# The first attention unit as a function of its own: 64x64 score tiles, a Q and a K tile per level, and K on ScalarE's DMA queue

## The chip, the cores and the metric

The kernel runs on one core of one Trainium2 chip. The metric is the device time of one execution in microseconds (us); the median of several runs counts. Engines are called as the profile calls them: PE (TensorE, its matmuls), PEld (its weight loads), DVE (VectorE), ACT (ScalarE), POOL (GpSimd) and SP (SyncE, which here only issues DMAs).

## The reference

Two blocks follow each other: a gated linear attention, and a small set of experts that all see every token.

```python
# q, k, v, alpha: (4, 8, 768, 48)  (batch, heads, sequence, head width)
for t in range(S):
    state = alpha[:, :, t, :, None] * state + einsum('bhd,bhe->bhde', k[:, :, t], v[:, :, t])
    y[:, :, t] = einsum('bhd,bhde->bhe', q[:, :, t], state)
x = y.transpose(0, 2, 1, 3).reshape(B * S, H * D)        # (3072, 384)
p = domain_probs / (domain_probs.sum(-1, keepdims=True) + 1e-09)   # (3072, 4)
for e in range(4):                                       # w1: (4, 384, 1024), w2: (4, 1024, 384)
    h = maximum(x @ w1[e], 0.0)
    out += p[:, e:e + 1] * (h @ w2[e])
```

All arrays are float32.

## The kernel before, in words

**Units and groups.** The sequence is cut into 6 blocks of 128 positions. One block of one batch element, with its 8 heads, is a unit; there are 24. A unit's result is 128 columns ("a slot") of the transposed expert input x. Units are gathered into groups: the first has 2 units, the others 4, the last 2. For each group and expert the kernel runs `up` (x times w1, in 8 chunks of 128 hidden features, L562 or L570) and `down` (hidden times w2, L663). The first group starts with unit 0 alone: `up(0, 0, fc, slice(0, 1))` for 8 chunks, then `down(0, 0, [0])`.

**A unit.** `attention(u)` is a generator; each `yield` ends a step. Raw alpha, K, Q and V lie with 128 positions on the partitions. TensorE turns alpha, K and Q, two heads (a "pair") at a time, so that the 2 x 64 padded features of a pair are on the partitions and positions in the free dimension (`turned`, L277): tiles `AT` (L288), `KT` (L293) and `QT` (L307) of 128 x 4 pairs x 128 positions. The decay between two positions is a product of alphas; it is built in 7 levels. On level li, blocks of 2^li positions are joined in pairs: the Q of the right block meets the K of the left one. `copy_q(li)` (L328, ScalarE) copies Q's right halves into a block `qb` in which the other head of the pair is zero; `next_q(li)` (L335, VectorE) multiplies the right halves of `QT`, in place, by the decay of the left block, and halves the decay tile (`dec`, L337); `next_k(li)` (L347, L348) copies one half of K into a new `KT` and multiplies the other. For unit 0 (`alone`) the copy is POOL's, for the others ScalarE's. `products(li)` (L355) computes scores: per pair and half of the block a matmul with 128 contraction rows, 64 stationary columns and 2 heads x 32 moving columns. `take(li)` (L365) puts them under a mask into `near` (two 64 x 64 diagonal blocks per head). The diagonal itself is the dot product of Q and K, made on VectorE (`own_terms`, L298 and L299, and L381). Level 6 gives the block between the two halves (`far`, L410). Both are copied into `lat` (L423, L428), and `result` (L450) multiplies V by it, 32 output features at a time in four strips; for later blocks a term with the running state is added. `turn_keys` (L475) and L489/L497 update that state.

**Features in a rearranged order.** x has 384 features, 48 per head. The order in which `result` lays them on 3 x 128 partitions is not the natural one: first 32 of each head, then the rest. So V is loaded in three DMAs (L179 to L181, for odd heads in swapped parts) and w1 in three DMAs per piece (L221 twice, L222) that gather its rows in the same order.

**Loads.** All of these are issued by SP, in program order: `load(0, "akqv")`, `load(1, "akqv")`, `p_all`, four pieces of w1 of expert 0 (`load_piece(0, i)`), and then whatever the steps ask for: unit 2's alpha, K and Q within unit 0's steps, the w2 pieces (L224) when `up` starts, unit 2's V, and the w1 pieces of expert 1. ScalarE's queue loads only `ident` and `masks`.

**Order.** The program's order is written out. In the head a list of (unit, n) pairs runs one step of a unit and then n idle matmuls (`fill`, L795), which multiply zeros; it takes unit 0 to its result and unit 1 through three steps. `norm_probs` (VectorE, L264 to L268) follows. After that, steps are kept in `waiting` with due times on a clock that counts estimated cost, and `advance` in the expert loops runs those that are due: 12 steps of unit 1 and the last 2 of unit 0 lie between the matmuls of the first slot. Every later unit is dealt out in the same way.

Of the kernel before, what the change touches and what calls it, by code (L numbers as in the profile page):

```python
# [20 lines left out]
def kernel(  # L21
# [46 lines left out]
    TAIL = D - QUAD  # L68
# [8 lines left out]
    assert DM == H * D and S % P == 0 and D == QUAD + HD // 4 and H == 8 and DM == 3 * P and NT <= 512 and H % 2 == 0  # L77
# [50 lines left out]
    values = [const.tile([P, H, HD], F32, name=f"rv{i}") for i in range(2)]  # L128
# [25 lines left out]
    in_pairs = range(half + 2 * B + 1, half + 4 * B)  # L154
    MARGIN = 6.0
# [11 lines left out]
    def load(u, names):  # L167
        if u >= len(units):
            return
        cb, b = units[u]  # L170
        for nm in names:
            src = srcs[nm][b, :, cb * P:(cb + 1) * P, :].rearrange("h s d -> s h d")
            if nm != "v":
                nc.sync.dma_start(out=raw(u, nm)[:, :, :D], in_=src)
                continue

            pairs = raw(u, nm).rearrange("p (a i) d -> p a i d", i=2)
            src = src.rearrange("p (a i) d -> p a i d", i=2)
            nc.sync.dma_start(out=pairs[:, :, 0, :D], in_=src[:, :, 0])  # L179
            nc.sync.dma_start(out=pairs[:, :, 1, :TAIL], in_=src[:, :, 1, QUAD:])  # L180
            nc.sync.dma_start(out=pairs[:, :, 1, TAIL:D], in_=src[:, :, 1, :QUAD])  # L181

# [12 lines left out]
    def load_piece(l, i, beside=False):  # L195
# [21 lines left out]
        if l == 0:  # L217
            heads = moe_w1[e].rearrange("(h d) f -> h d f", d=D)[:, :, c * QF:(c + 1) * QF]
            w = w.rearrange("p (c f) -> p c f", f=QF)
            for part in range(2):  # L220
                nc.sync.dma_start(out=w[:, part], in_=heads[part * H // 2:(part + 1) * H // 2, :QUAD])  # L221
            nc.sync.dma_start(out=w[:, 2], in_=heads[:, QUAD:])  # L222
# [56 lines left out]

    def attention(u):  # L280
# [8 lines left out]
        after = u + 2 if u == 0 else u + 1 if u > 1 else len(units)  # L289
# [13 lines left out]
        alone = u == 0  # L303
        if not alone:
            own_terms()
        yield
        nc.vector.tensor_mul(QT, turned(pair(rq)), AT)  # L307
        if alone:
# [31 lines left out]
        def next_k(li):  # L340
            m = LEVELS[li]
            old = new = halves(KTs[li], m)
            if li + 1 < len(LEVELS):
                KTs.append(keys())
                new = halves(KTs[-1], m)
                copy = nc.gpsimd.tensor_copy if alone else nc.scalar.copy
                copy(out=new[:, :, :, 1, :], in_=old[:, :, :, 1, :])  # L347
# [55 lines left out]
        next_q(6)  # L403
# [21 lines left out]
        for s in range(2):  # L425
            rows = slice(HALF * s, HALF * (s + 1))
            copy = nc.vector.tensor_copy if alone and s else nc.scalar.copy
            copy(out=lat[rows, :, rows], in_=near[rows])  # L428
# [437 lines left out]
```

## Time and profile before

| | before |
|---|---|
| median of 3 runs | 1052.53 us (1051.61 to 1052.69) |
| span of the profiled execution, first to last instruction | 1050.8 us |
| what the median has beyond that span | 1.7 us |
| PE busy | 1033.8 us (98%) in 8554 matmul instructions |
| DVE, ACT, POOL busy | 778.3, 565.7 and 37.7 us |
| bytes moved | 251.66 MB, mean 239 GB/s |
| granted TensorE clock | 1.000 |

The page lists the profiled execution by its span alone; its first instruction runs 0.24 us after the span's start, and the 1.7 us by which the median is longer lie outside of it. A matmul of float32 numbers is recorded as two matmul instructions; a transpose is one. The recorded duration of a matmul contains its way through the array, so a stream is read from start to start. "Idle before" names what released an engine; it is inferred from semaphores. A DMA instruction on SP lasts as long as its issue.

### The profile page before, as it was taken

How to read it: one execution, taken by the hardware profiler on the slowest of the kernel's cores; microseconds unless marked ns; L12 is line 12 of the kernel's file. 1: busy time of each engine (PE TensorE's matmuls, PEld its weight loads, DVE VectorE, ACT ScalarE, POOL GpSimd, SP SyncE). 2: the span in 40 equal slices, each digit the busy share in tenths (PEclk: the TensorE clock that was granted, in tenths of full speed). 3: DMA queues.
4: the chain of work that ended last, by engine and by line, in shares of the span. 5: the costliest groups of instructions: out<-in, count | busy, mean ns of one | idle time of the engine just before them, and what ended most of it. 6: DMA issues, size and time to landing. Idle time of an engine off the chain costs nothing.

```text
span 1050.8 us, 21723 instructions
## 1 busy us (share of the span) xinstructions
PE 1033.8 (98%) x8554; PEld 899.2 (86%) x8554; DVE 778.3 (74%) x1620; ACT 565.7 (54%) x1195; POOL 37.7 (4%) x81
## 2 busy tenths in 40 slices
PE   8899999999999999999999999999999999999998
PEld 8777777687787899898898998898989989898998
DVE  5588777668779868778877777987887875656565
ACT  4687876575657545447456436565474453323232
POOL 3000010000001000000000000000000000000000
PEclk9999999999999999999999999999999999999999
DMA  7596699997868949669669569577594454444531
GB/s 118 161 333 210 241 313 352 320 344 235 300 247 260 382 154 317 270 210 303 241 214 336 187 219 366 183 271 258 170 361 179 183 211 180 182 184 177 207 154 46
DMA packets 158549, 251.66 MB, mean 239 GB/s; under 512 B 120144, under 2 KB 134864, under 8 KB 135920
## 3 DMA queue, kind: packets, MB, share of 16 engines
q1 hardware_dynamic: 151984, 207.89, 58.7%
q0 software_dynamic: 6016, 42.08, 10.0%
q8 instruction: 67, 1.10, 0.4%
q10 hardware_dynamic: 448, 0.32, 0.1%
q14 instruction: 34, 0.28, 0.1%
HBM read 207.79 MB, written 42.47 MB: 238 GB/s over the span
## 4 chain that ended last, share of the span: by engine, by line
PE 85%; DVE 5%; ACT 4%; DMA 2%; issue 2%; SPq 1%; POOL 0%; ACTq 0%; DVEq 0%; POOLq 0%
PE ops L663 36%; PE one L570 23%; PE two L570 11%; PE sc L355 6%; PE yps L450 3%; PE tp L277 3%; ACT qb L328 2%; PE one L562 1%; PE sps L489 1%; DMA hT<-in_moe_w_dram 1%; PE far L410 1%; DVE hT L616 1%; DMA w<-in_moe_w_dram 1%; DVE near L365 1%; DVE QT L335 1%
## 5 line engine op out<-in xcount | busy, mean ns | idle before, releaser
L663 PE MATMUL ops<-w,hT 128*128 128x384 f32 x1872 | 342.7, 340 | 0.2 <-DVE hT L616 0.2
L663 PEld LDWEIGHTS ops<-w,hT 128*128 128x128 f32 x1872 | 322.6, 188 | 4.0 <-ACT t L581 0.6
L570 PE MATMUL one<-xT,w 128*128 128x512 f32 x960 | 251.8, 398 | 0.4 <-ACT t L581 0.4
L570 PEld LDWEIGHTS one<-xT,w 128*128 128x128 f32 x960 | 176.1, 188 | 38.3 <-ACT t L581 1.2
L581 ACT ACTIVATE t<-one 128x512 f32<-128x512 f32 (+1 forms) x192 | 106.7, 556 | 175.1 <-PE one L570 169.9
L328 ACT COPY qb<-QT 64x256 f32<-64x256 f32 x336 | 136.6, 407 | 58.2 <-DVE QT L335 30.3
L610 DVE SCALAR_TENSOR_TENSOR hT<-t,hT 128x512 fp32r<-128x512 f32 (+1 forms) x172 | 110.4, 642 | 63.3 <-ACT hT L608 62.0
L583 DVE TENSOR_TENSOR t<-t,two 128x512 f32<-128x512 f32 (+1 forms) x172 | 109.2, 635 | 53.2 <-PE two L570 32.0
L608 ACT ACTIVATE hT<-t 128x512 fp32r<-128x512 f32 (+1 forms) x172 | 101.8, 592 | 86.8 <-DVE t L583 86.2
L570 PE MATMUL two<-xT,w 128*128 128x512 f32 x480 | 136.5, 393 | 0.1
L570 PEld LDWEIGHTS two<-xT,w 128*128 128x128 f32 x480 | 90.0, 188 | 20.5 <-DVE acc L692 0.9
L663 PE MATMUL ops<-hT 128*128 128x384 f32 x288 | 100.8, 492 | 0.6 <-DMA hT<-in_moe_w_dram 0.3
L616 DVE SCALAR_TENSOR_TENSOR hT<-hT 128x512 fp32r<-128x512 f32 (+1 forms) x172 | 100.6, 634 | 0.0
L365 DVE COPY_PREDICATED near<-masks,sc 128x256 f32<-128x256 uint8 x144 | 77.0, 535 | 22.2 <-PE sc L355 19.3
L335 DVE TENSOR_TENSOR QT<-QT,dec 128x256 f32<-128x256 f32 x144 | 61.0, 423 | 38.8 <-ACT qb L328 38.3
L355 PEld LDWEIGHTS sc<-qb,KT 128*64 128x64 f32 x2304 | 72.7, 138 | 9.0 <-issue 4.4
L355 PE MATMUL sc<-qb,KT 128*64 128x64 f32 x2304 | 77.2, 223 | 2.6 <-ACT qb L328 2.6
L663 PEld LDWEIGHTS ops<-hT 128*128 128x128 f32 x288 | 52.1, 190 | 30.6 <-DMA hT<-in_moe_w_dram 1.2
L692 DVE SCALAR_TENSOR_TENSOR acc<-ops,p_all,acc 128x384 f32<-128x384 f32 x82 | 49.8, 614 | 27.2 <-PE ops L663 26.3
L347 ACT COPY KT<-KT 128x256 f32<-128x256 f32 x138 | 57.5, 417 | 5.1 <-PE sc L355 1.9
L348 DVE TENSOR_TENSOR KT<-KT,dec 128x256 f32<-128x256 f32 x144 | 60.0, 417 | 0.0
L562 PE MATMUL one<-xT,w 128*128 128x256 f32 (+1 forms) x240 | 46.7, 341 | 0.6 <-ACT xT L467 0.6
(90 smaller groups left out, 932.4 us busy)
## 6 DMA issues: line engine op xcount, KB each, us to landing
w<-kept SPq DMA_DIRECT2D x144, 1152.0 KB
kept<-w POOLq DMA_DIRECT2D x32, 1152.0 KB, 7.3
hT<-in_moe_w_dram SPq DMA_DIRECT2D x32, 384.0 KB
w<-in_moe_w_dram SPq DMA_DIRECT2D x48, 128.0 KB
ra<-in_alpha_dram SPq DMA_DIRECT2D x23, 192.0 KB
rk<-in_k_dram SPq DMA_DIRECT2D x23, 192.0 KB
rq<-in_q_dram SPq DMA_DIRECT2D x23, 192.0 KB
out_dram<-acc POOLq DMA_DIRECT2D x22, 192.0 KB, 7.0
```

The source lines that it names most:

```text
L328: nc.scalar.copy(out=qb[rows, :, i, :].rearrange("p a (b r) -> p a b r", r=m), in_=qv[rows])
L335: nc.vector.tensor_mul(qv, qv, spread(dv[:, :, :, 0], m))
L348: nc.vector.tensor_mul(new[:, :, :, 0, :], old[:, :, :, 0, :], spread(halved(decs[li])[:, :, :, 1], m))
L355: nc.tensor.matmul(out[HALF * s:HALF * (s + 1), 2 * p:2 * p + 2, :], lhsT=KTs[li][:, p, HALF * s:HALF * (s + 1)], rhs=qbs[li][:, p, :, QUA ...
L365: nc.vector.copy_predicated(near.rearrange("p a (b two r) -> p a b two r", two=2, r=m)[:, :, :, 1, :], mk.unsqueeze(1).broadcast_to([P, H, ...
L570: nc.tensor.matmul(out, lhsT=w[:, part, kc], rhs=x_part(gi, part, kc), start=(part == terms[0] and kc == 0), stop=(part == terms[-1] and k ...
L581: nc.scalar.activation(out=t, in_=one, func=ACT.Copy, scale=FINE)
L583: nc.vector.tensor_add(t, t, two)
L608: nc.scalar.activation(out=top, in_=x, func=ACT.Relu, scale=TRIM)
L610: nc.vector.scalar_tensor_tensor(out=low, in0=x, scalar=0.0, in1=top.bitcast(F32), op0=ALU.max, op1=ALU.subtract)
L616: nc.vector.scalar_tensor_tensor(out=dif, in0=top.bitcast(F32), scalar=1 / 4096.0, in1=low.bitcast(F32), op0=ALU.mult, op1=ALU.subtract)
L663: nc.tensor.matmul(sums[at], lhsT=h, rhs=w, start=(n == begins[at]), stop=(n == ends[at]))
```

## The change

Unit 0 gets a function of its own, `first_unit`; `attention` loses its branches for it.

- Each level of unit 0 has its own Q tile and its own K tile; these lie in the four buffers that later hold split w1 pieces. ScalarE copies Q's left halves from the old to the new tile (`same_q`), VectorE writes the right ones (`next_q`), POOL copies and VectorE multiplies K's halves (`next_k`).
- Scores are computed per head: 64 contraction rows, 64 stationary columns, 32 moving columns (64x64 tiles of the array), 16 matmuls a level in place of 8. No `qb` copies.
- The diagonal comes from 16 more matmuls of K with Q before any decay (`plain`), multiplied by the identity; Q is turned twice for that. `own_terms` is gone for unit 0.
- The result multiplies V by `diag` and `across` directly, without `lat`: 48 matmuls with 64 contraction rows and 32 columns, in place of 16 with 128 rows.
- Features are in natural order in all units: V has 32 zeros between heads (tiles of 80 columns a head), `result` takes strips across a head's end with two terms, and V and a w1 piece are one DMA each.
- K of unit 0 is issued by ScalarE's queue, between `ident` and `masks`; `p_all` is issued after the head, and `norm_probs` runs in the first slot's fifth chunk.
- The head's list has 13 entries instead of 18, and fewer idle matmuls (20 after the first 7, 42 before). Unit 1 has two steps in it instead of three; it has 13 among the first slot's matmuls instead of 12, due 0.75 of a slot earlier, and its `own_terms` come after Q's product.
- Units of a batch element's first block skip the last `next_q`.

```diff
-    values = [const.tile([P, H, HD], F32, name=f"rv{i}") for i in range(2)]
+    values = [const.tile([P, H, VD], F32, name=f"rv{i}") for i in range(2)]      # VD = D + QUAD
+    HEAD = [(0, 1), (0, 1), (0, 2), (0, 2), (0, 0), (0, 1), (0, 1), (1, 0), (0, 6), (0, 0), (1, 3), (0, 3), (0, 0)]
...
-    def load(u, names):
+    def load(u, names, queue=nc.sync):
...
-            nc.sync.dma_start(out=pairs[:, :, 0, :D], in_=src[:, :, 0])
-            nc.sync.dma_start(out=pairs[:, :, 1, :TAIL], in_=src[:, :, 1, QUAD:])
-            nc.sync.dma_start(out=pairs[:, :, 1, TAIL:D], in_=src[:, :, 1, :QUAD])
+            queue.dma_start(out=raw(u, nm)[:, :, :D], in_=src)
...
-            heads = moe_w1[e].rearrange("(h d) f -> h d f", d=D)[:, :, c * QF:(c + 1) * QF]
-            w = w.rearrange("p (c f) -> p c f", f=QF)
-            for part in range(2):
-                nc.sync.dma_start(out=w[:, part], in_=heads[part * H // 2:(part + 1) * H // 2, :QUAD])
-            nc.sync.dma_start(out=w[:, 2], in_=heads[:, QUAD:])
+            nc.sync.dma_start(
+                out=w.rearrange("p (c f) -> p c f", f=QF),
+                in_=moe_w1[e].rearrange("(c p) f -> p c f", p=P)[:, :, c * QF:(c + 1) * QF])
...
+    def first_unit():
...
+        def same_q(li):
+            old, new = (halves(t, LEVELS[li]) for t in QTs[li:li + 2])
+            nc.scalar.copy(out=new[:, :, :, 0, :], in_=old[:, :, :, 0, :])
+
+        def next_q(li):
+            old, new = (halves(t, LEVELS[li]) for t in QTs[li:li + 2])
+            nc.vector.tensor_mul(new[:, :, :, 1, :], old[:, :, :, 1, :],
+                                 spread(halved(decs[li])[:, :, :, 0], LEVELS[li]))
+
+        def next_k(li):
+            old = new = halves(KTs[li], LEVELS[li])
+            if li < 6:
+                new = halves(KTs[li + 1], LEVELS[li])
+                nc.gpsimd.tensor_copy(out=new[:, :, :, 1, :], in_=old[:, :, :, 1, :])
+            nc.vector.tensor_mul(new[:, :, :, 0, :], old[:, :, :, 0, :],
+                                 spread(halved(decs[li])[:, :, :, 1], LEVELS[li]))
+
+        def products(li, outs):
...
+            for p in range(NP):
+                for i in range(2):
+                    for s in range(2):
+                        nc.tensor.matmul(outs[i][keys[s], p].rearrange("p (b r) -> p b r", r=m),
+                                         lhsT=KTs[li][rows[i], p, keys[s]],
+                                         rhs=qv[rows[i], p, each * s:each * (s + 1), 1, :],
+                                         start=True, stop=True)
+
+        def take(li, outs):
...
+            for i in range(2):
+                nc.vector.copy_predicated(
+                    diag[:, NP * i:NP * (i + 1)].rearrange("p a (b two r) -> p a b two r", two=2, r=m)[:, :, :, 1, :],
...
+        nc.scalar.copy(out=AT, in_=turned(pair(ra)))
+        yield
+        tq = turned(pair(rq))
+        dec(0)
+        nc.vector.tensor_mul(QTs[0], tq, AT)
+        same_q(0)
+        next_q(0)
+        dec(1)
+        dec(2)
+        yield
+        nc.scalar.copy(out=KTs[0], in_=turned(pair(rk)))
+        yield
+        tq = turned(pair(rq))
+        yield
+        first = sc(P)
+        products(0, part(first, HALF))
+        same_q(1)
+        nc.scalar.copy(out=plain, in_=tq)
+        load(2, "akq")
+        next_q(1)
+        next_k(0)
+        same_q(2)
+        next_q(2)
+        yield
...                                   # products(1); the plain products and products(2); products(3)
+        next_k(3)
+        same_q(5)
+        next_q(5)
+        next_k(4)
+        next_k(5)
+        take(0, part(first, HALF))
+        take(1, part(first, HALF + QUAD))
+        yield
...                                   # far, take(2), take(3), two ScalarE copies of far into across
+        over = ps.tile([P, KC, HALF], F32, name="y2", tag="w")
+        products_of([(over, 0, across)])
+        nc.scalar.copy(out=xraws[0][:, :, HALF:P], in_=over)
+        third = sc(HALF)
+        products(4, part(third, 0))
+        products(5, part(third, QUAD))
+        take(4, part(third, 0))
+        take(5, part(third, QUAD))
+        next_k(6)
+        yield
+        low, high = (ps.tile([P, KC, HALF], F32, name=f"y{i}", tag="w") for i in range(2))
+        products_of([(low, 0, diag), (high, 1, diag)])
+        nc.scalar.copy(out=xraws[0][:, :, :HALF], in_=low)
+        nc.vector.tensor_add(xraws[0][:, :, HALF:P], xraws[0][:, :, HALF:P], high)
+        yield
...                                   # turn_keys and the state, as before
-        load(0, "akqv")
+        load(0, "aq")
+        load(0, "k", nc.scalar)
+        nc.scalar.dma_start(out=masks, in_=nc.inline_tensor(mask_np, name="masks_c").ap())
+        load(0, "v")
         load(1, "akqv")
-        nc.sync.dma_start(out=p_all, in_=moe_domain_probs.rearrange("(n p) e -> p n e", p=P))
...
-        runs = [attention(u) for u in range(len(groups[0]))]
+        runs = [first_unit(), attention(1)]
         fill(7)
...
-        norm_probs()
+        nc.sync.dma_start(out=p_all, in_=moe_domain_probs.rearrange("(n p) e -> p n e", p=P))
...
-        waiting.extend((span * (k + 1) / 15, u, runs[u])
-                       for k, u in enumerate([1, 1, 1, 0, 1, 0, *[1] * 8]))
+        waiting.extend((span * (k + 0.25) / 15, u, runs[u])
+                       for k, u in enumerate([1, 1, 1, 0, 1, 0, *[1] * 9]))
         for fc in range(FCH):
             up(0, 0, fc, slice(0, 1))
+            if fc == FCH // 2:
+                norm_probs()
             advance(cost(0, 0, 0) / 2)
```

## The prediction

> **What bounds the kernel now.** I read the page's busy shares first, then busy time by stage, then the timeline of the first 26 us, then one-matmul details. The stages:
>
> ```profile
> core 0: us, PE busy (x) PEld busy (x) DVE busy (x) ACT busy (x) POOL busy (x), PEclk, DMA share, GB/s
> 0.00:4.60 4.60, 3.35 (x14) 3.06 (x14) 0.00 (x0) 1.28 (x1) 3.95 (x17) 1.00 0.73 122
> 4.60:9.40 4.80, 4.72 (x32) 4.75 (x33) 0.74 (x2) 1.17 (x2) 2.40 (x6) 1.00 1.44 153
> 9.40:25.10 15.70, 13.79 (x215) 12.85 (x213) 13.93 (x39) 8.75 (x20) 2.35 (x5) 1.00 0.59 102
> 25.10:45.30 20.20, 18.22 (x214) 14.33 (x215) 10.47 (x30) 12.40 (x34) 0.00 (x0) 1.00 0.64 174
> ...
> 160.00:1050.00 890.00, 886.04 (x7012) 780.05 (x7009) 663.31 (x1356) 452.47 (x941) 20.87 (x39) 1.00 0.68 241
> ```
>
> From 160 us on TensorE stands still for 4 of 890 us: nothing there can be won by an earlier load or a shorter wait, and whatever the start saves or loses arrives at the end whole. TensorE's real work begins at 25.1 us; what fills it before is largely the idle matmuls of L795. So I price the stretch up to 25.1 us, then the 20 us in which unit 1 runs among the first slot's expert matmuls. The chain of the first unit:
>
> ```profile
> 8.66 0.69 DVE L307 TENSOR_TENSOR QT<-tp,AT 128x512 f32<-128x512 f32 x1 [8.66 <-PE tp L277]
> ...
> 9.44 0.88 ACT L328 COPY qb<-QT 64x256 f32<-64x256 f32 x2 [1.38 <-DVE QT L307]
> ...
> 10.35 0.42 DVE L335 TENSOR_TENSOR QT<-QT,AT 128x256 f32<-128x256 f32 x1
> ...
> 10.87 0.86 ACT L328 COPY qb<-QT 64x256 f32<-64x256 f32 x2 [0.55 <-DVE QT L335]
> ...
> 18.94 0.83 ACT L328 COPY qb<-QT 64x256 f32<-64x256 f32 x2
> ...
> 23.44 1.08 PE L450 MATMUL yps<-lat,rv 128*32 128x128 f32 x32
> ...
> 25.11 3.62 PE L562 MATMUL one<-xT,w 128*128 128x128 f32 x30 [0.59 <-ACT xT L467]
> ```
>
> Q is updated in place, so each level is a relay: ScalarE copies two halves (0.86 us), VectorE multiplies (0.42 us). Seven copies start between 9.44 and 18.94, a period of 9.5/6 = 1.58 us, stretched by VectorE's other work. After the last come scores, masks, two copies into lat, 16 matmuls and a copy: 25.1.
>
> **Part 1, the relay goes.** With a Q and a K tile per level, ScalarE's copy of one half and VectorE's product of the other both read the old tile and write the new one, so neither waits for the other: a level costs VectorE its own two products. I add VectorE's work from start to start where rows follow without waiting (10.35, 10.70, 11.03: 0.34 us for 256 columns; 0.20, 0.13, 0.10, 0.08 for the shorter decs). Q's first product 0.60; eleven products of Q and K at 0.34, 3.7; decs 1 to 5, 0.6; two multiplications by the identity, half as wide as L381's 0.69, 0.7; twelve masked copies of 128 columns, where before has six of 256. A pair of those took 1.29 us for levels 0 and 1 (15.61 to the next start at 16.90) and 0.81 later, so 0.65 and 0.40 each; half the width with 0.12 kept as fixed cost gives 0.38 and 0.26: 4 x 0.38 + 8 x 0.26 = 3.6. Sum 9.2 us. Gone are own_terms (1.1) and the lat copies; the product of K with plain Q on TensorE replaces the former. K's last product (0.4) goes after the masks, before the final addition.
>
> Start: the three loads it needs, with ident and masks, are 713 KB. In windows of one microsecond the first six moved 0, 24, 228, 207, 171 and 161 KB, so all have passed by 5.5, whichever queue issues them. Alpha, ident and masks (319 KB) had passed by 3.3 and were used at 4.65, 1.3 later; so the last of the three is usable near 6.8. Alpha shares the engines with K now and may land 0.6 later; against that Q's transposes wait for one idle matmul instead of five and K's transposes. I put Q's first product at 7.5 instead of 8.66. 7.5 + 9.2 = 16.7 if VectorE never waits. Laying the rows in program order I find waits: 0.4 for K's copy (ScalarE does it after Q's first copy, done 9.25), 0.4 around the plain product, 0.55 for the scores of levels 4 and 5, which TensorE computes only after the far block's result: masks end near 18.1. Then 32 result matmuls 0.45 + 0.25 to drain, a copy or addition 0.4, 0.1 to the first expert matmul: 19.3. I add 0.9 for semaphore steps that the rows do not resolve: **20.2 instead of 25.1, so -4.9**.
>
> Cover: POOL's six K copies (0.42) run beside VectorE's products; uncovered they would cost up to 6 x 0.4 = 2.4. ScalarE has about 7 us of copies in these 12 us. Idle matmuls now are 14 after the first scores, 3.0 us, each in front of something TensorE must await anyway.
>
> **Part 2, the small tiles on TensorE.** 336 matmul instructions in 64x64 or 64x32 tiles: no row of this trace has tiles of 64 rows. Nearest:
>
> ```profile
> 20.33 1.13 PE L355 MATMUL sc<-qb,KT 128*64 128x64 f32 x32
> 33.40 2.08 PE L355 MATMUL sc<-qb,KT 128*64 128x64 f32 x64
> ```
>
> 32 more cost 0.95 us: 30 ns each, and the idle matmuls, 128 wide, took 115 ns (42 in 4.85); half the columns would be 57 alone, so two column tiles run together. L450's tiles of 32 columns, 128 moving: 1.08 us for 32, 34 each, four together. If row tiles run together like column tiles, a level of 32 instructions costs about 0.45; if not, 0.85. I take 0.45, since both rows show full overlap, and keep 0.85 for the range: seven such blocks (six levels and plain Q) and the last 64 result instructions are then 0.4 longer each, 3.2, of which TensorE's present waits take up about 0.8: 2.4 later, 22.6. Lower than 0.45 gains nothing: VectorE then paces.
>
> The Trainium skill speaks against this part: "TensorEngine Tiling (Array Packing)", section "Instruction Overhead", puts about 60 cycles on every matmul and advises not to take a tiling factor from a dimension that is already small; the scores here move 32 columns. As an estimate from that page, 60 cycles at 2.4 GHz are 25 ns, 0.8 a block, six blocks 0.35 longer, 2.1 less the same 0.8: the time would be 1048.5. No run here has moved 32 columns.
>
> **Part 3, loads.** K on ScalarE's queue takes an issue of 0.56 us there, ahead of the masks' issue and the table load (1.28) that must be done by AT's copy near 6: covered, 0. V becomes one DMA of three (about 1.2 us of issue saved per unit on SP), p_all goes behind the head. The expert weights L221/L222, three DMAs a piece, become one. Their rate now, beside that of the second weights, whose shape the new DMA has:
>
> ```profile
> 14.00:25.00 11.00, 9.19 (x170) 8.41 (x166) 10.09 (x29) 5.90 (x14) 1.53 (x3) 1.00 0.32 102
> 31.00:36.00 5.00, 4.05 (x80) 3.76 (x80) 3.98 (x11) 3.53 (x11) 0.00 (x0) 1.00 0.98 275
> ```
>
> At 102 GB/s the first 1.5 MB need 15 us, and TensorE waits for them near 30 us. At 275 they need 5.7, behind unit 1's loads (which end about 12.5, where the one-microsecond windows fall from 128 to 30 GB/s): there by 19, just ahead of 20.2. If the rate stayed at 102 they would be there by 28, 3 us after the seventh chunk wants them. SP's next: unit 2's loads, p_all, the second weights; the fourth of these waits for unit 1's own_terms, now after the head, but is wanted 10 us later.
>
> **Part 4, unit 1 among the experts (25.1 to 45.3).** It enters one step poorer: four transposes (0.45 on TensorE), Q's product and own_terms (1.8 on VectorE) now lie behind the first expert chunk, so its relay starts at +2.3 us instead of +1.8; behind own_terms queues its next Q product, for which ScalarE's next copy waits. norm_probs (1.2, formerly at 23.2) sits between two levels where VectorE waits for ScalarE. Against that fall the weight waits: about 0.7 for L221's pieces at 30 to 31, 0.34 for the second weights at 35.8. ScalarE's queue up to the fourth level's copies holds 8 evictions of 0.28, four pairs of 0.85 and 1.9 of other copies, 7.5; two evictions come before +2.3, so it ends at +9.2 and the fourth level's scores at +9.9 instead of +10.4 (35.48). **-0.4**, between -1.2 and +1.2.
>
> **Part 5, the other 22 units.** The result still has 28 matmuls for a unit with a past and 16 without, four strips at a time; skipped next_q(6) is off the path. 0; by 1.08 us a result, 5% either way in order effects would be 1.2.
>
> Sum: 1050.8 - 4.9 - 0.4 = 1045.5 for the profile's span. The median shown, 1052.53, is 1.7 above that span, which I keep: **1047.2**.
>
> **Rivals.** (a) Row tiles do not overlap, or the weights stay slow: 2.4 to 3 less gain, 1049.9. For: no row shows them; against: columns do. (b) The head's gain is given back in part 4, ScalarE being 12.4 of 20.2 us busy there and the relay longer than the TensorE work around it: 1052. It needs 4 us of new waits; TensorE had only 2 there. (c) Slower: TensorE's half clock. The first 14 idle matmuls took 3.35 us, 239 ns each, the later 42 115 ns; after 7.2 us it was up, following six busy us. The change leaves 12 idle instructions behind its first four steps where there were 28, and waits between. If the speed-up fails to come, 8.2 us of TensorE work in the head (4.3 in small tiles, 3.0 idle, 0.9 transposes) double, less 2.5 of slack, and the first experts lose 2: the start comes at about 26, the time is 1055. It decides once over 5.3 us are lost. Against: TensorE would still be busy about four fifths of 4.6 to 9.3, and the trace keeps the full pace through a wait of 1.33 us at 19.87.
>
> **Numbers.** The forecast 0.62 (its own range 1044.5 to 1049.6); (a) 0.16; (b) 0.10; (c) 0.12. A measurement of this kernel can tell about 0.2% (2.1 us) from no change: faster 0.77, same 0.11, slower 0.12. The range takes the forecast's lower end and goes up through most of (a): 1044.5 to 1051.5.
>
> **What would show it.** Right: L562's first matmul near 20; Q levels 0.4 to 0.8 us apart; a 32-instruction score block under 0.7 us; no L562 wait for w; the stage up to the first slot's last matmul still about 20 us; beyond 160 us the same 4 us of TensorE idle. Wrong: score blocks of 0.9 us or more, VectorE waiting for sc; matmuls of 240 ns after 8 us; L562 waiting for DMA; over 22 us from the first expert matmul to the slot's end; any difference past 160 us.

## The result and the profile after

The changed kernel takes 1053.87 us (median of 11 runs, 1052.96 to 1056.17), the kernel before 1052.5 beside it (1051.61 to 1053.48): the ratio is 1.0018, its 95% interval 1.001 to 1.0025. It is slower by 0.2%, where 1047.2 was forecast with a range up to 1051.5. The profiled execution took 1056.11 us, of which the span is 1054.3. It is one of the longer ones: seven of the eleven times lie from 1053.0 to 1053.9 and four from 1055.4 to 1056.2.

The stages of the kernel after, as they were shown of the kernel before (busy time and number of instructions of each engine, granted clock, share and rate of the DMA engines):

```profile
core 0: us, PE busy (x) PEld busy (x) DVE busy (x) ACT busy (x) POOL busy (x), PEclk, DMA share, GB/s
4.60:9.40 4.80, 3.54 (x17) 3.27 (x18) 1.44 (x3) 0.91 (x2) 2.19 (x6) 1.00 1.51 170
...
9.40:25.10 15.70, 13.07 (x385) 11.66 (x384) 9.49 (x32) 5.26 (x13) 3.16 (x6) 1.00 1.04 208
...
160.00:1050.00 890.00, 889.40 (x7005) 778.21 (x7003) 662.58 (x1354) 451.77 (x939) 20.87 (x39) 1.00 0.66 240
```

Read the second stage first. VectorE fell from 13.93 to 9.49 us and ScalarE from 8.75 to 5.26: the relay is gone, as Part 1 said, though some 3.0 us of VectorE's part is work that only moved behind this stage (`norm_probs`, and unit 1's Q product and `own_terms`). TensorE has 385 matmuls instead of 215, and the DMA engines are full (1.04 instead of 0.59, at 208 instead of 102 GB/s), as Part 3 wanted. In the last stage TensorE stands still for 0.6 us instead of 4, and yet the kernel ends later. TensorE's own timeline of the head (start, duration, engine, line, operation, how many, and in brackets the idle time before it with what ended it):

```profile
7.23 1.09 PE L267 MATMUL tp<-ident,rq 128*128 128x128 f32 x4 [1.26 <-DMA rq<-in_q_dram]
...
8.54 1.06 PE L267 MATMUL tp<-ident,rk 128*128 128x128 f32 x4
...
10.24 0.78 PE L267 MATMUL tp<-ident,rq 128*128 128x128 f32 x4
...
11.40 0.67 PE L320 MATMUL sc<-QT,w 64*64 64x32 f32 x32
11.89 0.65 PE L320 MATMUL sc<-w,w 64*64 64x32 f32 x32
...
15.40 1.38 PE L957 MATMUL idle<-st 128*128 128x128 f32 x10
18.74 0.49 PE L957 MATMUL idle<-st 128*128 128x128 f32 x2 [1.96 <-issue]
19.16 0.68 PE L395 MATMUL far<-w,w 64*64 64x64 f32 x16
...
23.84 0.60 PE L957 MATMUL idle<-st 128*128 128x128 f32 x4 [0.68 <-issue]
24.37 0.86 PE L416 MATMUL y<-w,rv 64*32 64x64 f32 x64
25.82 0.91 PE L723 MATMUL one<-xT,w 128*128 128x128 f32 x6 [0.59 <-ACT xT L433]
```

The first expert matmul (called T0 below) starts at 25.82, not at 20.2, and not even at the 25.11 of before. Two holes, 1.96 and 0.68 us, lie in the middle of idle matmuls, which wait for no data; the view of waits calls both "issue" (nothing that the profile shows was waited for). VectorE meanwhile stands idle:

```profile
8.35 0.69 DVE L342 TENSOR_TENSOR QT<-tp,AT 128x512 f32<-128x512 f32 x1 [1.73 <-PE tp L267]
...
22.78 0.89 DVE L330 COPY_PREDICATED w<-masks,sc 128x128 f32<-128x128 uint8 x4 [4.35 <-PE sc L320]
```

The second part of the loss is spread over the rest of the program. The groups from 160 to 1050 us, first before, then after (`one` and `two` are the sums of `up`, `ops` those of `down`; how many, busy time, mean duration of one):

```profile
L663 PE MATMUL ops<-w,hT 128*128 128x384 f32 x1872 | 342.7, 340 | 0.2 <-DVE hT L616 0.2
L570 PE MATMUL one<-xT,w 128*128 128x512 f32 x960 | 251.8, 398 | 0.4 <-ACT t L581 0.4
L570 PE MATMUL two<-xT,w 128*128 128x512 f32 x480 | 136.5, 393 | 0.1
```

```profile
L824 PE MATMUL ops<-w,hT 128*128 128x384 f32 x1872 | 342.7, 339 | 0.2 <-DVE hT L777 0.2
L731 PE MATMUL one<-xT,w 128*128 128x512 f32 x960 | 254.7, 400 | 0.4 <-ACT t L742 0.2 <-DVE t L464 0.2
L731 PE MATMUL two<-xT,w 128*128 128x512 f32 x480 | 138.1, 396 | 0.0
```

The same 1440 matmuls of `up`, in lines that the change does not touch, are busy 4.5 us longer; those of `down` are not. From the start of one such matmul to the start of the next the median went from 230 to 234 ns for `one` and from 229 to 234 for `two`. Laying ScalarE's evictions `hT` (the results of `up`) of both traces side by side in their order gives the account of the spans: after is behind by 0.68 us when the experts begin, by 0.27 at 47 us and 0.24 at 107, is ahead by 0.94 at 147, and then loses steadily until it is behind by 3.49 at the end: 4.4 us in some 890.

So two things had to be explained, each with a theory and a rival. **The holes.** Theory F: TensorE runs out of instructions. They are loaded from memory too; the page's queue of instruction loads whose count fits TensorE's moved

```profile
q8 instruction: 67, 1.10, 0.4%
```

packets, MB and share before, and in the kernel after

```profile
q8 instruction: 69, 1.13, 0.4%
```

With 8554 and 8714 matmuls and as many weight loads, a packet is 16 KB and serves 255 and 253 instructions. 64x64 tiles take twice the matmuls, and a weight load for each, so the head uses packets up faster, while the DMA engines that bring them are full. Rival V: VectorE's chain and the late Q bind the head, and the holes are a symptom. **The drift.** Theory P: the pace of `up` depends on where xT lies in SBUF. The V tiles have become 512 bytes a partition longer each, which alone shifts nothing modulo 128, but the order in which the tiles are allocated is another: xT begins 64 bytes past a multiple of 128, not 96, and w1 32 past one, as before. Rival: late weights or something else that lasts on from the head.

### The profile page after: what moved, and what is told of

Its sections match the earlier page's. It is cut to its first block, busy times and chain, and to the rows that moved or that the text cites. A ratio compares the mean times of both kernels' runs of the same rounds, so it can differ in the third digit from the quotient of the medians.

```text
span 1054.3 us, 21938 instructions
## 1 busy us (share of the span) xinstructions
PE 1036.4 (98%) x8714; PEld 896.2 (85%) x8714; DVE 776.9 (74%) x1617; ACT 562.4 (53%) x1188; POOL 38.3 (4%) x81
## 3 DMA queue, kind: packets, MB, share of 16 engines
q0 software_dynamic: 6016, 42.08, 10.1%
## 4 chain that ended last, share of the span: by engine, by line
PE 89%; DVE 4%; ACT 4%; issue 2%; DMA 1%; SPq 0%; DVEq 0%; ACTq 0%
PE ops L824 37%; PE one L731 23%; PE two L731 11%; PE sc L520 6%; PE tp L267 3%; PE yps L615 3%; PE one L723 1%; ACT qb L494 1%; PE far L576 1%; PE sps L650 1%; DMA hT<-in_moe_w_dram 1%; DVE w L227 1%; PE idle L957 1%; DMA rq<-in_q_dram 1%; DVE near L530 1%
## 5 line engine op out<-in xcount | busy, mean ns | idle before, releaser
L731 PE MATMUL one<-xT,w 128*128 128x512 f32 x960 | 254.7, 400 | 0.4 <-ACT t L742 0.2
L494 ACT COPY qb<-QT 64x256 f32<-64x256 f32 x322 | 130.9, 407 | 53.4 <-DVE QT L501 29.6
L530 DVE COPY_PREDICATED near<-masks,sc 128x256 f32<-128x256 uint8 x138 | 73.7, 534 | 23.9 <-PE sc L520 21.2
L501 DVE TENSOR_TENSOR QT<-QT,dec 128x256 f32<-128x256 f32 x135 | 56.8, 421 | 35.4 <-ACT qb L494 34.9
L520 PEld LDWEIGHTS sc<-qb,KT 128*64 128x64 f32 x2208 | 69.6, 138 | 8.9 <-issue 4.7
L520 PE MATMUL sc<-qb,KT 128*64 128x64 f32 x2208 | 74.0, 223 | 2.6 <-ACT qb L494 2.6
L513 DVE TENSOR_TENSOR KT<-KT,dec 128x256 f32<-128x256 f32 x138 | 57.6, 417 | 0.0
```

The source lines that it names most:

```text
L494: nc.scalar.copy(out=qb[rows, :, i, :].rearrange("p a (b r) -> p a b r", r=m), in_=qv[rows])
L513: nc.vector.tensor_mul(new[:, :, :, 0, :], old[:, :, :, 0, :], spread(halved(decs[li])[:, :, :, 1], m))
L520: nc.tensor.matmul(out[HALF * s:HALF * (s + 1), 2 * p:2 * p + 2, :], lhsT=KTs[li][:, p, HALF * s:HALF * (s + 1)], rhs=qbs[li][:, p, :, QUA ...
L530: nc.vector.copy_predicated(near.rearrange("p a (b two r) -> p a b two r", two=2, r=m)[:, :, :, 1, :], mk.unsqueeze(1).broadcast_to([P, H, ...
L731: nc.tensor.matmul(out, lhsT=w[:, part, kc], rhs=x_part(gi, part, kc), start=(part == terms[0] and kc == 0), stop=(part == terms[-1] and k ...
```

## The experiments on the drift

**xT moved, by 32 bytes in the kernel after and by 96 in the kernel before.**

```diff
+        work.tile([P, 8], F32, name="gap", bufs=1)        # 32 bytes; before: [P, 24]
         xTs[0] = work.tile([P, 3, KC, NT], F32R, name="xT", bufs=1)
+        work.tile([P, 24], F32, name="rest", bufs=1)      # before: [P, 8]
```

> Changed kernel; only the place of xT in SBUF differs: an unused 32-byte tile in front of it and 96 bytes behind it put xT at byte 96 of a 128-byte line, as in the kernel before (the change moved it to byte 64), while every other operand that TensorE reads keeps its place within a line. Theory P (the place of xT sets the pace of the matmuls that read it): the 1440 matmuls one and two <-xT from 160 us on fall from about 234 to about 230 ns from start to start, the stretch from 160 us to the end shortens by 4 to 4.5 us of 890, and the time is 1049 to 1051. Rival W (the pace fell because weights and V now arrive in other transfers, or because of the order of the features): nothing changes, 1053 to 1056. In both the head stays as it is, first expert matmul at about 25.8 us.

> Kernel before; only the place of xT differs: 96 unused bytes in front of it and 32 behind put it at byte 64 of a 128-byte line, where the changed kernel has it. Theory P: one and two <-xT go from about 230 to about 234 ns, the time rises by 4 to 4.5 us to 1056.5. Rival W: nothing changes, 1052.5. The head stays, first expert matmul at 25.1.

In `after_xT_up32` the median is 1051.72 us, ratio to before 0.9995 (0.9982 to 1.0008), and the pace is 230 and 229 ns again:

```profile
L733 PE MATMUL one<-xT,w 128*128 128x512 f32 x960 | 251.7, 398 | 0.5 <-ACT t L744 0.4 <-DMA w<-kept 0.2
L733 PE MATMUL two<-xT,w 128*128 128x512 f32 x480 | 136.3, 392 | 0.1
```

The time is above the 1049 to 1051 expected: `ops` went from 173 to 174 ns, and from 147 us on the evictions still lose 1.6 us. A shift by 96 bytes, to where the kernel after has xT modulo 128, gives the kernel before the slow pace, 234 and 235 ns, and 1061.92 us, ratio 1.0088 (1.0073 to 1.0103):

```profile
L572 PE MATMUL one<-xT,w 128*128 128x512 f32 x960 | 255.9, 402 | 0.2 <-ACT t L583 0.2
L572 PE MATMUL two<-xT,w 128*128 128x512 f32 x480 | 138.5, 397 | 0.0
```

No arithmetic, load or order differs: theory P is shown in both directions. The loss of the second run is larger than expected, and `down` slowed as well: `ops` from 173 to 176 ns from start to start, 5.6 us over 1872 of them. The tiles behind xT had moved too, among them hT, which `down` reads. Where xT was moved by 32 bytes and hT by 512 (`after_head_light` below and the three runs built on it), `ops` stays at 173 ns, and from 147 us on the evictions gain 0.1 to 0.7 us on those of before, where the kernel after loses 4.4: the place of xT accounts for the whole drift.

**Other places.** The kernel after, run once each with gaps of 64 and 96 bytes ahead of xT and the sum kept at 512, and with 32 bytes ahead and nothing behind (so that hT moves by 32).

> The kernel after, with an unused tile of 64 bytes a partition ahead of xT and one of 448 behind it: xT begins 64 bytes later (96 bytes past the place of w1, modulo 128), and hT and w2 keep their places modulo 512. The head of the program is unchanged. Theory P (the pace of the up matmuls goes by where xT lies in SBUF beside w1): one<-xT,w starts neither at the 234 ns of the kernel after nor must it be the 230 of the run with 32 bytes; if only the distance of xT from w1 modulo 64 counts, it is that of 32 bytes (230) and 64 bytes is again 234. Rival (drift from something that lasts from the head, such as late weights): 234 whatever the gap. Head: T0 between 22.8 and 25.8 us as in the runs so far.

> The same with 96 bytes ahead of xT and 416 behind it: xT lies at the same place as w1 modulo 128. If the distance modulo 64 counts: 64 bytes and 0 bytes of gap agree, and 32 and 96 agree, with 230 ns for the latter two. If the distance modulo 128 counts, the four gaps give a series with one best place, perhaps below 230. Rival: 234 whatever the gap.

> The kernel after with 32 bytes ahead of xT and nothing behind it, so that hT moves by 32 bytes as well, against w2 which stays. Theory P: one and two at 230 ns as in the run with xT alone moved, and ops<-w,hT leaves its 173 ns (in the run of the kernel before with 96 and 32 bytes it went to 176, and there hT had also moved against w2), some 480 x 3 ns per side of the second matmuls more. Rival: ops stays at 173, and what made 176 in that run was the pace of the first matmuls alone.

| xT moved by | start of xT, modulo 128 (w1 starts at 32 throughout) | `one`, `two` start to start | `ops` |
|---|---|---|---|
| 0 (after) | 64 | 234, 234 ns | 173 ns |
| 32 | 96 | 230, 229 | 174 (hT moved by 128) |
| 64 | 0 | 232, 231 | 173 |
| 96 | 32 | 232, 232 | 173 |
| 32, hT moved by 32 | 96 | 231, 229 | 175 |
| kernel before | 96 | 230, 229 | 173 |
| before, moved by 96 | 64 | 234, 235 | 176 (hT moved by 128) |

Equal starts modulo 128 gave paces within 1 ns of each other in two different kernels; modulo 64 alone does not fit (0 and 64 bytes of gap differ). w1 lay at the same place modulo 128 in every run, so whether the place of xT counts by itself or its distance from w1, which the theory named, is open; so is why 96 is the best start. `ops` leaves its 173 ns in the three runs that moved hT, and all else behind xT, by 32 or 128 bytes, and keeps it in the runs that moved them by 512. The three times (1053.46, 1054.70 and 1054.07 us, one each) hold the head's variation as well and decide nothing.

## The experiments on the head

**How many instructions had passed when TensorE stopped.** This needs no kernel of its own: the windows from the start to the hole count them. The kernel after, up to the first and up to the second hole:

```profile
0.00:16.60 16.60, 14.13 (x220) 13.17 (x220) 7.89 (x23) 5.81 (x11) 9.20 (x27) 1.00 1.17 205
0.00:23.00 23.00, 18.57 (x346) 16.99 (x347) 9.94 (x31) 7.44 (x15) 9.30 (x27) 1.00 1.10 181
```

220 + 220 and 346 + 347 matmuls and weight loads: 253 instructions lie between the holes, one packet. (With those that this view leaves out TensorE stands behind some 449 and 705 instructions, and the expectations use these numbers.) Now a kernel with the first entry of the head's list at (0, 4) instead of (0, 1), six idle matmul instructions more between the transposes of alpha and those of Q:

> Changed kernel with 4 idle matmuls instead of 1 between the transposes of alpha and of Q. Theory C (TensorE was at half pace until 10 us because it stood idle from 6 to 7.2 us): the transposes of K take about 0.6 us instead of 1.06, those of Q up to 0.5 less, K's first tile is ready about 0.8 us earlier and the first expert matmul moves up by 0.5 to 1 us, less what the stalls at 16.8 and 23.2 us take back. Rival: the pace does not rise earlier and nothing else moves: 0 to +0.3 us in the head. The pace of one and two <-xT stays at 234 ns in both.

```profile
0.00:16.00 16.00, 12.11 (x220) 11.05 (x220) 7.67 (x22) 5.63 (x11) 8.92 (x27) 1.00 1.15 199
```

```profile
4.34 0.63 PE L267 MATMUL tp<-ident,ra 128*128 128x128 f32 x4
...
7.85 0.63 PE L267 MATMUL tp<-ident,rq 128*128 128x128 f32 x4 [1.99 <-DMA rq<-in_q_dram]
...
17.34 1.73 PE L957 MATMUL idle<-st 128*128 128x128 f32 x8 [1.91 <-issue]
19.00 1.12 PE L395 MATMUL far<-w,w 64*64 64x64 f32 x16
```

The hole came after 440 instructions again, six matmuls earlier in the program (behind 4 of the 12 idle ones instead of 10). What stops TensorE is a count, not a place in the program. Theory C of this run, that idle time ahead of Q keeps the pace at half, stays open: the pace was full already at 4.34, ahead of the added matmuls, Q came only at 7.85, and behind the hole the pace was half (216 ns for an idle matmul, `far` 1.12 us instead of 0.68), which it was not behind the hole of the kernel after. T0 was 26.04, the time 1055.72 us (ratio 1.0026, 1.0017 to 1.0036).

In the kernel after, the packet that ends the first hole was moved from 15.97 to 17.11 us and TensorE went on at 18.74; none was moved between 11.7 and 15.9, while the engines moved 337 GB/s of data. In the kernel before one passed from 13.84 to 14.98 us, amid 56 GB/s, and one from 22.42, and TensorE did not stand for issue in the head.

**Data out of the way.** w1 pieces 1 to 3 wait for a one-column memset by POOL that stands behind its third copy of K (11.6 us); unit 2's loads go behind the head.

```diff
-        load(2, "akq")                                    # in first_unit's fourth step
+        for i in range(1, NQ):                            # behind next_k(2)
+            load_piece(0, i, hold=True)                   # nc.gpsimd.memset(w[:, :1], 0.0) first
...
+        load(2, "akq")                                    # behind the head's loop
```

> Changed kernel; the first w1 pieces 1 to 3 wait for a POOL memset behind the level-2 copy of K (about 13 us), and unit 2's alpha, K and Q are issued behind the head. Theory F (TensorE ran out of instructions at 16.8 us because the transfer that brings the next ones lay behind the data transfers that SP had issued far ahead): the 1.96 us of idle with the releaser issue between two idle matmuls at 16.8 us go, far starts near 17 instead of 19.16, and the first expert matmul near 23.5 instead of 25.8, if no second stall grows; the time falls by about 2. Rival V (TensorE would have waited for VectorE there anyway): far stays at 19, the first expert matmul at 25.8, the same time. A piece that lands too late would show as a wait of L723 for w.

```profile
14.38 1.63 PE L959 MATMUL idle<-st 128*128 128x128 f32 x12
16.06 0.68 PE L398 MATMUL far<-w,w 64*64 64x64 f32 x16
...
22.26 0.60 PE L959 MATMUL idle<-st 128*128 128x128 f32 x4 [2.19 <-issue]
...
24.50 1.62 PE L726 MATMUL one<-xT,w 128*128 128x128 f32 x6 [0.59 <-ACT xT L436]
```

The first hole is gone and `far` starts 3.1 us earlier. The second, where those held pieces now run, grew from 0.68 to 2.19 us. T0 is 24.50; the time 1055.59 us (1.0032, 1.002 to 1.0044), with the slow place of xT. The supply follows the transfers, as F says; the time, expected to fall by about 2 us, did not.

**Fewer idle matmuls.** The same with most of the later idle matmuls left out and xT moved by 32 bytes.

```diff
-    HEAD = [..., (0, 0), (0, 1), (0, 1), (1, 0), (0, 6), (0, 0), (1, 3), (0, 3), (0, 0)]
+    HEAD = [..., (0, 0), (0, 0), (0, 0), (1, 0), (0, 3), (0, 0), (1, 0), (0, 0), (0, 0)]
```

> The kernel after with fewer instructions of TensorE in the head (idle matmuls from the sixth place of the head's order on 3 in all instead of 15 entries' worth: (0,0) where it was (0,1), (1,0) for (1,3), (0,3) for (0,6), (0,0) for (0,3)), the w1 pieces 1 to 3 issued after the second key is in and unit 2's a, k and q after the head, and xT moved by 32 bytes with hT in place modulo 512. Theory F (TensorE's instruction supply: a refill of 256 instructions comes late beside the transfers and TensorE runs dry): no stall named issue over 0.3 us before the first expert matmul, which starts at 21.5 to 22.5 us, later paces 230 and 173, time 1047 to 1049.5 us. Rival V (the head is bound by VectorE's chain and the late Q, the stalls are a symptom): T0 24 us or more, time 1050.5 to 1052. A third outcome: without the idle matmuls the clock falls to half and far and across take twice their time; T0 then 23 to 24.5.

```profile
22.00 0.95 PE L421 MATMUL y<-w,rv 64*32 64x64 f32 x46 [2.04 <-issue]
23.54 1.62 PE L728 MATMUL one<-xT,w 128*128 128x128 f32 x6 [0.59 <-ACT xT L438]
```

1051.00 us, ratio 0.9981 (0.997 to 0.9992). F's numbers missed: the second hole was not avoided but met in the result's matmuls, 2.04 us behind 346 + 346 instructions, and T0 (23.54) and the time fell into what the rival or the third outcome allowed. By the time alone F would have lost here; the count spoke for it.

**The transfers moved once more.** The memset goes behind POOL's last copy of K (15.3 us), so that the queues are empty when the second packet is due.

> The run after_head_light with the w1 pieces 1 to 3 held back further, until ScalarE's neighbour POOL has copied the last key (about 15.3 us instead of 11.6), so that no data is in the queues when TensorE's 449th instruction is reached (15.4 us). Theory F (refills of 256 instructions that come late beside data): the stall of 2.0 us at TensorE's 705th instruction goes or falls under 0.4 us, the first expert matmul starts at 21 to 22 us (23.5 in after_head_light), the time is 1048 to 1050 us. Rival (the stalls at 449 and 705 have nothing to do with the data transfers): a stall of about 2 us at 705 again, T0 23 to 24, time 1050.5 to 1051.5. A loss that both allow: the last pieces of w1 land at 19.5 to 21.5 us and a matmul waits for w, under 1 us.

```profile
19.07 1.93 PE L322 MATMUL sc<-w,w 64*64 64x32 f32 x64
21.87 1.25 PE L421 MATMUL y<-w,rv 64*32 64x64 f32 x64 [0.87 <-DVE w L332]
```

No hole is left before T0, with the same instructions on TensorE. T0 still was 23.72, within the rival's bounds and not F's 21 to 22: in this execution Q was used only at 7.70, and the small tiles ran slower from 16 us on (`far` 0.83, 64 scores 1.93 us instead of 1.14). A slower TensorE also needs its packet later, so the missing hole alone does not decide against the rival (the holes have nothing to do with the transfers). The packets do, in the runs whose hole at the 449th instruction is short or missing. The second packet was moved 3.4 us after that instruction in `after_head_light`, 3.8 in `after_k_behind_q` (below) and 4.0 in `after_loads_later`, with the DMA engines full in between, and 4.3 in `after_head_gap_kq` (below), with the engines busy 0.7 of the time. It was moved 1.8 us after it here (busy 0.4), 1.2 in `after_wide_fill` (below, idle) and 0.2 in the kernel before (0.5). With data in the way the packet comes later, and the rival is out; at the pace of `after_head_light` a hole of some 0.4 us might have been left (an estimate: it reached the 705th instruction 4.1 us after the 449th, and went on 1.5 us after its packet had passed). The time is 1050.04 us, ratio 0.9975 (0.9966 to 0.9984).

**K behind Q.** One line of the change undone, in the kernel after by itself and in the run above.

```diff
-        load(0, "aq")
-        load(0, "k", nc.scalar)
+        load(0, "aqk")
```

> The kernel after with this one part of the change undone: K issued third on SyncE's queue, behind Q, instead of on ScalarE's. Read for the landing of Q and K: Q 6.2 to 6.6 us if K beside it takes its bandwidth, 7.0 to 7.1 if not. Stalls of TensorE at the 449th and, if not met, the 705th instruction again (1 to 2.3 us), the 234 ns pace of the up matmuls again, time 1052.5 to 1055.5 us.

> The run after_head_gap with K taken back from ScalarE's queue and issued third on SyncE's, behind Q. If the load of K beside Q is what kept Q from coming earlier (Q lands at 7.0 to 7.1 us in the kernels before and after alike), Q lands at 6.2 to 6.6 and K at 7.2 to 7.6; Q's transposes start up to 0.6 us earlier, K's wait instead, and the first score products, which need both, start where they did: T0 within 0.5 us of after_head_gap, time within 1 us of it. If the DMA engines share by rows whatever the queue, Q lands at 7.0 again and K later: T0 0.5 to 1 us later.

The issues of the first 3 us (KB, and us from issue to landing), after and with K behind Q:

```profile
rk<-in_k_dram ACTq DMA_DIRECT2D x1, 192.0 KB, 5.2
rq<-in_q_dram SPq DMA_DIRECT2D x1, 192.0 KB, 5.8
```

```profile
rq<-in_q_dram SPq DMA_DIRECT2D x1, 192.0 KB, 4.4
rk<-in_k_dram SPq DMA_DIRECT2D x1, 192.0 KB, 4.9
```

K beside Q makes Q land 1.4 us later. Q's transposes started at 5.80 instead of 7.23. K itself, issued 0.7 us later, landed 0.4 us later, but its transposes, which follow Q's, started at 6.94 instead of 8.54: both gained, more than expected. The Trainium skill, "DMA: Bandwidth & Descriptors", section "Queues, rings and completion order", says that each DMA engine takes turns between the queues that have work for it; the two durations agree with that. T0 was 22.55 in the one run (1053.55 us, a single execution, with the slow place of xT) and 22.87 in the other (1048.77 us, ratio 0.9971, 0.996 to 0.9981). Holes of 0.44 and 1.50 us stayed in the one, and holes of 0.24 and 0.88 us were back in the other: a head that runs earlier needs its packets earlier.

**All of it together, and the clock kept.** The idle matmuls of the kernel after again, but in the three longest places as 384 columns each, a third as many; the w1 pieces held until VectorE has taken level 3.

```diff
+            wide = DM if n in (3, 6) else P
+            for _ in range(n // 3 if wide == DM else n):
+                nc.tensor.matmul(idle[:, :wide], lhsT=zeros[:, :P], rhs=zeros[:, :wide],
+                                 start=True, stop=True)
```

> The run after_head_gap_kq with the idle matmuls of the kernel after again, but those of its three longest places as matmuls of 384 columns, a third as many (so that TensorE's clock is kept up with fewer instructions), and the w1 pieces 1 to 3 held back until VectorE has taken the last masked level (about 17 us). Theory F: no stall named issue over 0.4 us at TensorE's 449th or 705th instruction; with the clock kept at full speed the first expert matmul starts at 20.3 to 21.5 us, its first fc block at the full pace (six matmuls in about 0.9 us instead of 1.6), the time is 1046.5 to 1048.5 us. Rival (the supply of instructions cannot keep up with 64x64 tiles at the full clock whatever else is in the queues): a stall of 0.8 us or more at 449 or 705, T0 at 22 us or later, time 1048.5 to 1050.5.

```profile
5.96 1.00 PE L269 MATMUL tp<-ident,rq 128*128 128x128 f32 x4
...
13.18 1.56 PE L961 MATMUL idle<-st 128*128 128x384 f32 x4
14.71 0.68 PE L396 MATMUL far<-w,w 64*64 64x64 f32 x16
...
19.15 1.00 PE L421 MATMUL y<-w,rv 64*32 64x64 f32 x64
20.74 0.91 PE L728 MATMUL one<-xT,w 128*128 128x128 f32 x6 [0.59 <-ACT xT L438]
```

No hole, the full pace from 7.14 us on but for a short stretch ahead of the result (1.00 us for 64 matmuls instead of 0.86), T0 at 20.74: 1048.20 us, ratio 0.9959 (0.9945 to 0.9972), inside what F expected and the lowest median of all. 64x64 tiles can be fed, so the rival (supply too slow whatever else runs) is out. Of the 4.4 us that this head wins, 2.9 are given back in the first slot: by ScalarE's evictions the lead falls from 4.39 to 1.50 us at 47 us. Before, the largest wait between the first slot's matmuls was

```profile
PE far L410 <- ACT qb L328: 0.8, 1, 0.8
```

and here it is

```profile
PE far L581 <- ACT qb L499: 2.4, 1, 2.4
```

ScalarE's `qb` copies are late here because VectorE is, and VectorE because of a load:

```profile
28.08 0.25 DVE L256 TENSOR_REDUCE tot<-p_all 128x24 f32<-128x96 f32 x1 [1.83 <-DMA p_all<-in_moe_domain_probs_dram]
...
29.84 0.82 ACT L499 COPY qb<-QT 64x256 f32<-64x256 f32 x2 [1.28 <-DVE QT L506]
...
38.66 3.28 PE L829 MATMUL ops<-hT 128*128 128x384 f32 x6
```

`norm_probs` stands 1.83 us for `p_all`, which this order of loads issues at 22.20 instead of 18.07 (`after_xT_up32`). So VectorE's next product of Q starts at 29.34, where `after_xT_up32`, with its T0 2.1 us later, has it at 29.49. Behind the wait of 2.4 us TensorE is slower as well; the same six `ops` take there

```profile
38.30 2.20 PE L826 MATMUL ops<-hT 128*128 128x384 f32 x6
```

How much of the lead an earlier `p_all` would keep was not run.

## Why the prediction was wrong

- **Part 1, T0 at 20.2 (-4.9): failed in the kernel as changed (+0.7), and nearly right with its obstacles gone (20.74).** The sum of VectorE's work was sound: in `after_wide_fill` its rows run from 7.00 to 16.34 without a long wait, with four more masked copies later, 10.1 us in all against 9.2. That T0 came so near has some luck in it: Q's first product came at 7.00, 0.5 us ahead of the forecast, and VectorE stood 1.89 us for the scores of levels 4 and 5, where 0.55 was put. In the kernel as changed three terms were missed. The step that took the idle matmuls as "each in front of something TensorE must await anyway", and the one that priced the small tiles, went by their time and counted neither as instructions that must be loaded: 2.64 us of holes. The step "all have passed by 5.5, whichever queue issues them" took the three loads as one sum and let Q land when the sum allowed; Q's first product came at 8.35, not 7.5, and the order of issue was worth 1.4 us of Q's landing. And the transposes of Q and K ran at half pace (1.09 and 1.06 instead of 0.60 us). The holes and Q's delay make 3.5 of the 5.6 us that Part 1 missed; the rest was not taken apart.
- **Rival (c), half pace,** came in part: in the kernel after the four transposes at 7.23 take 1.09 us and only from about 10.2 on is the pace full; before it was full after 7.2. It is not fixed by the program: the head of `after_xT_up32`, which differs by an unused tile, had full pace at 6.91 us (0.63) and T0 at 22.82, with holes of 0.85 and 0.41. The Trainium skill, "TensorE: Matmul & The Clock Gate", Part 1, says that the clock gate watches a window that runs freely and so changes at another moment from run to run; that agrees. It may be why the times of this kernel fall in two bunches; that is not shown, for there is one trace of it.
- **Part 2 was right.** A block of 32 scores starts 0.49 us after the one before it (11.40 to 11.89), against 0.45 taken. The estimate of 0.8 worked out from the Trainium skill, "TensorEngine Tiling (Array Packing)", section "Instruction Overhead", is not what the trace shows: 0.49 / 32 is 15 ns a matmul. But the step asked only how long such a block takes TensorE; that it also uses 64 instructions of a supply of about 254 a packet was on no line of the sum.
- **Part 3 was right on the weights** (no expert matmul waits for w). The 0 for K on ScalarE's queue was wrong, as said: it counted the issue and not the share of the DMA engines. And the faster weights, with unit 2's loads (one run moved both), are what stood in the way of the instruction packets: the gain of one part was the cost of the other.
- **Part 4, -0.4: right,** 0.68 to 0.27 is -0.41, and it is -0.40 to -0.43 in the five other runs whose experts start at the full pace and do not wait for `p_all`, also where the lead is 2.3 us (`after_xT_up32`). Up to there nothing is given back, against rival (b). In `after_wide_fill`, with a lead of 4.4 us, 2.9 are; but what is seen to cost them is the late `p_all` and TensorE's slower pace behind the wait, not ScalarE's load, which rival (b) named. Whether a lead of 4.4 us, as Part 1 forecast it, would be kept without these is not shown.
- **Part 5, 0: failed.** From 147 us on the kernel loses 4.4 us. The step looked at the instructions of the other units, which are the same, and not at where their operands lie: xT has moved. The end of the text ruled out "any difference past 160 us". Between 107 and 147 us it gains 1.2; in that stretch of the kernel before TensorE waits 0.5 for QT and 0.4 for hT, waits that are gone after. That the skipped last `next_q` does this was not tried.

By the spans: +0.7 in the head, -0.4 in the first slot, -1.2 up to 147 us, +4.4 after, together +3.5 us (1050.8 to 1054.3), where -5.3 was forecast: 5.6 of the 8.8 us between are Part 1's, 3.2 Part 5's. The medians differ by 1.4 only, since the profiled execution of after is a long one, 2.2 us above its median. If the stretches behind the head are the same in every execution, which one trace cannot show, the experts of the median execution begin some 1.5 us ahead of before, at about 23.6 (an estimate from these times), and Part 1 missed by some 3.4 us there.

## What to carry to other kernels

Count instructions, not only time: where many small matmuls run beside heavy loads, find how many instructions a packet of the instruction queue serves, and see whether a packet is due while the queues are full; where idle matmuls are wanted, few wide ones use fewer instructions than many narrow ones. When a change adds or resizes a tile, every later tile moves: compare the start-to-start pace of untouched matmuls in both traces before looking for a reason in the edit, and try a gap of 32 bytes. Loads that go out together share the DMA engines (Q took 5.8 us beside K, 4.4 ahead of it), so what is needed first goes first; and where loads are held back, look which later step waits for what now queues behind them, as `norm_probs` did here.

## What the runs showed of the hardware that was not expected

- TensorE stood for 0.2 to 2.2 us behind 440 or about 693 of its counted instructions in ten of the twelve runs of this head, whatever instruction came next; the packet of instructions that it stood for had come late beside data (3.4 to 4.3 us instead of 0.2 to 1.8 us after the 449th instruction, in the runs compared above).
- A `one<-xT,w` matmul of 128x512 started every 230 to 234 ns depending on where xT starts modulo 128 bytes (96: 230; 0 and 32: 232; 64: 234), with w1 at 32 in every run; over the program that is some 4 to 5 us.
- The view of the granted clock read 1.00 for the stage from 4.6 to 9.4 us of the kernel after, in which four transposes took 1.06 to 1.09 us instead of 0.60: there the pace must be read from the rows.
